# Idle matmuls of one wait replaced by groups of several lengths and offsets, and copies of zeros on the other engines

## The chip, the cores and the metric

The kernel runs on one core of a Trainium2 chip. The core has five engines that work side by side and meet through semaphores: TensorE (matmul, PE in the profile, its weight loads PEld), VectorE (DVE), ScalarE (ACT), GpSimd (POOL) and SyncE (SP), which issues all transfers here. The metric is the device time of one execution in microseconds (us), the median over the runs. Smaller is better.

## The reference

A spectral layer over 8 batches of 3008 positions with 256 channels is followed by a feed-forward layer of width 2048. Cut to what is computed:

```python
X = np.fft.rfft(x, axis=1)
Yr = Xr @ w_r - Xi @ w_i + b_r
Yi = Xr @ w_i + Xi @ w_r + b_i
Yr = np.sign(Yr) * np.maximum(np.abs(Yr) - 0.01, 0.0)      # Yi likewise
y = np.fft.irfft(Yr + 1j * Yi, n=3008, axis=1)
h = y.reshape(-1, 256) @ w_in
out = (h - np.tanh(h)) @ w_out
```

The feed-forward weights come as 64-bit floats and are turned into pairs of 32-bit numbers on the chip.

## The kernel before

The Fourier transform is done by matmuls with constant matrices, in two steps of 47 and 64 (3008 = 47 × 64). `Forward` is the first step: it takes 4 of 32 pairs of rows, splits them into a high and a low part (L90 on ScalarE, L91 on VectorE), multiplies by `f1` (L215 to L217) and writes the result `st` to the DRAM tile `a` (L231, L234). `Spectrum`, for batch 0 `WholeSpectrum`, is the second step with the complex linear layer and the shrinking: it loads `at` from `a` (L255), multiplies by `f2` (L264), and for batch 0 adds the bias by a matmul (L346) and multiplies by the linear weights (L352); then follow the shrinking (L361 to L371), the inverse step (L375) and a store to `z`. A `Chunk` takes 470 positions (the last two 282) through the rest of the inverse transform (L407) and the feed-forward layer (L420 to L445).

TensorE works in two types. Operands of type float32r are numbers rounded to fewer bits; the kernel splits each into high and low and adds three products (L215 to L217, L284, L420, L445). Operands of plain float32 (L264, L352, L375, L407) are used whole.

The order is written out by hand: each engine runs its instructions in the order in which the code issues them (`tc.manual_schedule`), and the tile pools add the waits. Batch 0 has nothing to hide behind. Its `Forward` loop (L523 to L535) runs 16 steps, each with one idle matmul behind its three; at the end the `a` tile has to go out to DRAM and come back as `at`. In this wait stands `idle(16)` (L536). `idle(n)` (L504 to L507) takes a PSUM tile of pool `ps_h`, which has two, and multiplies a tile of zeros, `warm`, by itself n times over 512 columns, in float32r. Nobody reads the result.

Behind the wait, in program order: the first two loads of `at` (L577, L578), `combine_linear` (L117 to L127: sums of the linear weights on VectorE and GpSimd, `ones` and the bias row), the split of `i1`, and the loop over the 12 units (L581 to L613), in which the feed-forward weights are also converted, a few steps at a time, into `win_h`, `win_l`, `wout_h` and `wout_l`. These four tiles are written there for the first time.

Of the kernel before, what the change touches and what calls it, by code (L numbers as in the profile page):

```python
# [10 lines left out]
F32 = mybir.dt.float32  # L11
# [3 lines left out]
ALU = mybir.AluOpType  # L15
# [6 lines left out]
def index_maps():  # L22
    n = np.arange(S)
    time = np.zeros((64, 47), np.int64)
    time[n % 64, n % 47] = n
    starts = []
    for j in range(NJ):
        low = (47 * np.arange(64) + 64 * j) % S < S // 2
        starts.append(next(m for m in range(64) if low[m] and not low[m - 1]))
    return time, starts  # L30
# [36 lines left out]
def spectral_ffn(ctx, tc, x, w_r, w_i, b_r, b_i, w_in, w_out, f1, f2, i1, i2, out):  # L67
    nc = tc.nc
    P = 128
    w_in, w_out = w_in.bitcast(U32), w_out.bitcast(U32)  # L70
    _, m0 = index_maps()
# [11 lines left out]
    ps_h = ctx.enter_context(tc.tile_pool(name="ps_h", bufs=2, space=PSUM))  # L83
# [46 lines left out]
    win_h = const.tile([P, 2, FF], F32R, name="win_h")  # L130
    win_l = const.tile([P, 2, FF], F32R, name="win_l")
    wout_h = const.tile([P, NF, D], F32R, name="wout_h")
# [365 lines left out]
    with tc.manual_schedule(engines={E.PE, E.Activation, E.DVE, E.Pool, E.SP}):  # L498
        zero = cvt.tile([P, 512], F32, name="zero", tag="w_f")
# [4 lines left out]
        def idle(n):  # L504
            ps = ps_h.tile([P, 512], F32, name="idle", tag="h")
            for _ in range(n):
                nc.tensor.matmul(ps, warm[:, :P], warm, start=True, stop=True)  # L507

        idle(11)
        shifts = const.tile([P, 2], F32, name="shifts")  # L510
        below, rebias = shifts[:, 0:1], shifts[:, 1:2]
# [11 lines left out]
        for i in range(len(steps) + 2):  # L523
# [9 lines left out]
            if i >= 2:  # L533
                f, q = steps[i - 2]
                f.keep(q, nc.vector.tensor_copy if i % 3 == 0 else nc.scalar.copy)  # L535
        idle(16)  # L536
        units = [WholeSpectrum(0, jp) for jp in range(NJ // 2)]
        i2t = const.tile([96, NP * 94], F32, name="i2")
        lin = []
# [144 lines left out]
    for c in range(FIRST, NCH):  # L684
        at = NF * (c - 1)
# [35 lines left out]
```

## Time and profile before

| | us |
|---|---|
| runs | 2694.08 and 2696.0, median 2695.04 |
| span of the profiled execution | 2694.1 |
| TensorE busy, of the span | 2676.7 |
| VectorE, ScalarE, GpSimd busy | 1748.3, 1377.5, 2.0 |
| mean granted clock of TensorE | 0.998 |

Times in views are counted from the first instruction. A row of the timeline has start, length, engine, line, operation, output and inputs, sizes and a count; instructions of one kind that follow each other are merged into one row, whose length runs from the first start to the last end. In brackets stands how long the engine was idle before it, and what ended that. A row of the chain has start, length and what the end of the program is traced back to at that time. A granted clock of 1.00 is full speed. A matmul's own length is longer than the distance between two of them, since they overlap.

The edited place is near the start: `Forward` of batch 0 ends at 22.3 us and the first unit begins at 32.2 us. All of the about 2,584 us after the loop of units, from 110 us on, are chunks, with the other batches' transforms between them.

### The profile page before, as it was taken

The numbers are of one execution on the slowest core, as the hardware profiler recorded it, in microseconds if no ns is written. First come the engines' busy times: TensorE is split into PE (matmuls) and PEld (weight loads), VectorE is DVE, ScalarE is ACT, GpSimd is POOL, SyncE is SP. The second block draws the span as 40 slices with busy tenths as digits, with TensorE's granted clock in tenths as the row PEclk, the third lists the DMA queues.
The fourth block names the chain that finished last, engine by engine and source line by source line (L and its number), as shares of the span: only waits on it lengthen the run. The fifth ranks groups of instructions, "written<-read, shape, count | busy, mean of one in ns | idle before, by whom it ended". The sixth has DMA issues, their size and how long they took to land.

```text
span 2694.1 us, 36955 instructions
## 1 busy us (share of the span) xinstructions
PE 2676.7 (99%) x14169; PEld 2391.6 (89%) x14169; DVE 1748.3 (65%) x3079; ACT 1377.5 (51%) x2587; POOL 2.0 (0%) x5
## 2 busy tenths in 40 slices
PE   8999999999999999999999999999999999999999
PEld 6788988999889998999988999899988999998989
DVE  6895786666557666566755667666665666655555
ACT  5555555454554446454455445644455444444445
POOL 0000000000000000000000000000000000000000
PEclk9999999999999999999999999999999999999999
DMA  6423223110231103111022110411113111100000
GB/s 196 141 75 106 65 83 109 46 54 26 69 90 43 50 32 111 57 47 46 24 81 80 46 46 31 118 56 50 39 39 108 50 39 41 35 23 22 20 20 17
DMA packets 105135, 163.47 MB, mean 61 GB/s; under 512 B 7488, under 2 KB 70976, under 8 KB 104864
## 3 DMA queue, kind: packets, MB, share of 16 engines
q1 hardware_dynamic: 104960, 161.13, 19.8%
q8 instruction: 111, 1.82, 0.3%
q14 instruction: 64, 0.52, 0.1%
HBM read 86.13 MB, written 74.97 MB: 60 GB/s over the span
## 4 chain that ended last, share of the span: by engine, by line
PE 94%; DVE 3%; DMA 1%; ACT 1%; issue 1%; SPq 0%; DVEq 0%; ACTq 0%
PE o L445 37%; PE h L420 37%; PE ps_v L284 4%; PE ps_i L407 4%; PE ps_f L264 3%; PE ps_t L284 2%; PE ps_f L215 1%; PE ps_f L217 1%; PE ps_f L216 1%; PE ps_v L352 1%; DVE g L425 1%; PE ps_i L320 1%; PE ps_i L321 1%; PE ps_i L319 1%; DVE gl L433 0%
## 5 line engine op out<-in xcount | busy, mean ns | idle before, releaser
L425 DVE TENSOR_TENSOR g<-h,th 128x470 f32<-128x470 f32 (+1 forms) x832 | 532.2, 640 | 540.0 <-ACT th L423 531.9
L423 ACT ACTIVATE th<-h 128x470 f32<-128x470 f32 (+1 forms) x832 | 463.9, 558 | 757.3 <-PE h L420 756.3
L433 DVE TENSOR_TENSOR gl<-g,gh 128x470 fp32r<-128x470 f32 (+1 forms) x832 | 531.9, 639 | 285.8 <-ACT gh L427 203.2
L427 ACT CAST gh<-g 128x470 fp32r<-128x470 f32 (+1 forms) x832 | 483.0, 581 | 408.6 <-DVE g L425 401.2
L445 PE MATMUL o<-gh,wout_l 128*128 128x470 f32 (+1 forms) x1664 | 631.3, 379 | 1.1 <-ACT gh L427 1.1
L445 PE MATMUL o<-gl,wout_h 128*128 128x470 f32 (+1 forms) x1664 | 616.1, 370 | 1.1 <-DVE gl L433 1.1
L445 PE MATMUL o<-gh,wout_h 128*128 128x470 f32 (+1 forms) x1664 | 615.8, 370 | 0.0
L420 PE MATMUL h<-yl,win_h 128*128 128x470 f32 (+1 forms) x1664 | 480.7, 370 | 0.0
L420 PE MATMUL h<-yh,win_l 128*128 128x470 f32 (+1 forms) x1664 | 480.1, 370 | 0.0
L420 PE MATMUL h<-yh,win_h 128*128 128x470 f32 (+1 forms) x1664 | 479.5, 369 | 0.0
L445 PEld LDWEIGHTS o<-gl,wout_h 128*128 128x128 f32 x1664 | 312.8, 188 | 40.8 <-DVE gl L433 2.1
L445 PEld LDWEIGHTS o<-gh,wout_l 128*128 128x128 f32 x1664 | 313.1, 188 | 35.1 <-ACT gh L427 1.7
L420 PEld LDWEIGHTS h<-yh,win_l 128*128 128x128 f32 x1664 | 310.5, 188 | 36.2 <-ACT yh L411 0.4
L420 PEld LDWEIGHTS h<-yl,win_h 128*128 128x128 f32 x1664 | 310.6, 188 | 35.5
L420 PEld LDWEIGHTS h<-yh,win_h 128*128 128x128 f32 x1664 | 310.6, 188 | 35.5
L445 PEld LDWEIGHTS o<-gh,wout_h 128*128 128x128 f32 x1664 | 313.5, 188 | 32.0
L309 DVE TENSOR_TENSOR y<-tb,ps_v 64x256 f32<-64x256 f32 x384 | 160.2, 417 | 12.0 <-ACT tb L356 6.8
L407 PEld LDWEIGHTS ps_i<-i,zin 96*128 96x128 f32 x1024 | 126.1, 192 | 5.0 <-DVE st L231 1.0
L407 PE MATMUL ps_i<-i,zin 96*128 96x94 f32 x1024 | 128.0, 272 | 1.0 <-DVE st L231 0.8
L91 DVE TENSOR_TENSOR x_l<-xt,x_h 94x512 fp32r<-94x512 f32 x126 | 85.6, 686 | 46.2 <-ACT x_h L90 44.3
L264 PEld LDWEIGHTS ps_f<-f,at 128*128 128x128 f32 x768 | 101.5, 192 | 13.6 <-issue 8.2
L264 PE MATMUL ps_f<-f,at 128*128 128x128 f32 x768 | 103.1, 277 | 5.7 <-DMA at<-a 5.7
(98 smaller groups left out, 2077.8 us busy)
## 6 DMA issues: line engine op xcount, KB each, us to landing
xt<-in_x SPq DMA_DIRECT2D x64, 384.0 KB, 3.6
at<-a SPq DMA_DIRECT2D x96, 256.0 KB, 2.8
z<-zo SPq DMA_DIRECT2D x96, 256.0 KB, 2.0
out<-ot SPq DMA_DIRECT2D x50, 470.0 KB, 2.9
a<-st SPq DMA_DIRECT2D x56, 384.0 KB, 3.2
zin<-z SPq DMA_DIRECT2D x44, 480.0 KB, 4.2
w_raw<-in_moe_w_in SPq DMA_DIRECT2D x8, 512.0 KB, 4.6
w_raw<-in_moe_w_out SPq DMA_DIRECT2D x8, 512.0 KB, 5.1
```

The costliest lines, as they stand in the source:

```text
L91: rest.tensor_tensor(out=lo, in0=src, in1=hi.bitcast(F32), op=ALU.subtract)
L215: nc.tensor.matmul(pv, f1h, xl, start=True, stop=False)
L264: nc.tensor.matmul(pv[:, t, jj], self.at[:, jj, t * P:(t + 1) * P], rhs, start=True, stop=True)
L284: nc.tensor.matmul(dst, lhs[:, t], rhs[:, t, :], start=n == 0, stop=n == 5)
L309: nc.vector.tensor_tensor(out=y[ri * 64:(ri + 1) * 64, jj, :], in0=common(jj, ri), in1=self.vv[jj * 64:(jj + 1) * 64, ri * D:(ri + 1) * D] ...
L407: nc.tensor.matmul(ps[:, k * 94:(k + 1) * 94], self.zt[:, k, t * P:(t + 1) * P], i2t[:, p * 94:(p + 1) * 94], start=True, stop=True,)
L420: nc.tensor.matmul(h[:, :n], lhs[:, t, f * P:(f + 1) * P], rhs[:, t, :n], start=k == 0, stop=k == 5)
L423: nc.scalar.activation(out=th[:, :n], in_=h[:, :n], func=AF.Tanh)
L425: nc.vector.tensor_tensor(out=g[:, :n], in0=h[:, :n], in1=th[:, :n], op=ALU.subtract)
L427: nc.scalar.copy(out=gh[:, :n], in_=g[:, :n])
L433: nc.vector.tensor_tensor(out=gl[:, :n], in0=g[:, :n], in1=gh[:, :n].bitcast(F32), op=ALU.subtract)
L445: nc.tensor.matmul(self.o[t][:, :n], lhs[:, f, t * P:(t + 1) * P], rhs[:, :n], start=f == 0 and k == 0, stop=f == NF - 1 and k == 2,)
```

## The change

`idle(16)` at L536 becomes a call of a new function, `measure()`. It writes zeros into parts of `win_h` and `win_l` with copies on VectorE and ScalarE, and uses them as weights (`wt`, four blocks of 128 columns in turn) and as moving operand (`mv`). After `idle(8)` come three loops of float32r matmuls: 12 each of 470, 500, 504, 512 and 128 columns, those of 470 from elements 8, 0, 4 and 12 of `mv`; 24 each of 250, 252, 256, 236 and again 252 columns; and 24 each of 252 and 128 columns with the same block of weights throughout. These are 264 matmuls, in groups of six that add up in one of two PSUM tiles of pool `ps_h`. Then `idle(2)`. Last come eight subtractions of zeros on GpSimd, eight on VectorE and eight copies of zeros on ScalarE, of 252 and 504 columns, into parts of `win_l` and `wout_h`. All results are overwritten later or never read.

```diff
+        def measure():
+            wt = win_h.rearrange("p k f -> p (k f)")
+            mv = win_l.rearrange("p k f -> p (k f)")
+            nc.vector.tensor_copy(out=wt[:, :512], in_=zero)
+            nc.vector.tensor_copy(out=mv[:, :512], in_=zero)
+            nc.scalar.copy(out=mv[:, 512:1024], in_=zero)
+            pa, pb = (ps_h.tile([P, 512], F32, name=f"idle{v}", tag="h") for v in "ab")
+            idle(8)
+            for n, start in ((470, 8), (470, 0), (470, 4), (470, 12), (500, 8), (504, 8), (512, 8), (128, 8)):
+                for k in range(12):
+                    nc.tensor.matmul((pa, pb)[k // 6][:, :n], wt[:, k % 4 * P:(k % 4 + 1) * P], mv[:, start:start + n], start=k % 6 == 0, stop=k % 6 == 5)
+            for n, start in ((250, 8), (252, 8), (256, 8), (236, 8), (252, 0)):
+                for k in range(24):
+                    at = 256 * (k // 6 % 2)
+                    nc.tensor.matmul((pa, pb)[k // 12][:, at:at + n], wt[:, k % 4 * P:(k % 4 + 1) * P], mv[:, start:start + n], start=k % 6 == 0, stop=k % 6 == 5)
+            for n, same in ((252, 1), (128, 1)):
+                for k in range(24):
+                    at = 256 * (k // 6 % 2)
+                    nc.tensor.matmul((pa, pb)[k // 12][:, at:at + n], wt[:, :P], mv[:, 8:8 + n], start=k % 6 == 0, stop=k % 6 == 5)
+            idle(2)
+            sums = win_l[:, 1, :1024]
+            for n in (252, 504):
+                for _ in range(4):
+                    nc.gpsimd.tensor_tensor(out=sums[:, :n], in0=zero[:, :n], in1=zero[:, :n], op=ALU.subtract)
+            for n in (252, 504):
+                for _ in range(4):
+                    nc.vector.tensor_tensor(out=sums[:, 512:512 + n], in0=zero[:, :n], in1=zero[:, :n], op=ALU.subtract)
+            for n in (252, 504):
+                for _ in range(4):
+                    nc.scalar.copy(out=wout_h[:, :2].rearrange("p t e -> p (t e)")[:, :n], in_=zero[:, :n])
...
-        idle(16)
+        measure()
```

In the rows below, which are an engine's instructions in their order, a name ending in `_49` is the semaphore of the engine or transfer queue that is waited for. TensorE in the wait of batch 0, before: the last product of `Forward` (`ps_f_336`), the idle matmuls, and the two `f2` products of the first units.

```order
L217 MATMUL ps_f_336<-x_7_1_h,f_h 96x512
L507 MATMUL idle<-warm 128x512 [waits PE_49] x2
L507 MATMUL idle<-warm 128x512 x15
L264 MATMUL ps_f_393<-f_129,at 128x2x64 [waits DMAHW7_49,DMAHW1_49]
L264 MATMUL ps_f_393<-f_129,at 128x2x64 x3
L264 MATMUL ps_f_404<-f_129,at 128x2x64 [waits DMAHW0_49,DVE_49]
```

TensorE at the same place, now: the end of the groups and the same first unit (`ps_f_681` was `ps_f_393`).

```order
L523 MATMUL idleb<-win_l,win_h 128x252 x12
L527 MATMUL idlea<-win_l,win_h 128x252 x12
L527 MATMUL idleb<-win_l,win_h 128x252 x12
L527 MATMUL idlea<-win_l,win_h 128x128 x12
L527 MATMUL idleb<-win_l,win_h 128x128 x12
L507 MATMUL idle<-warm 128x512 [waits PE_49]
L507 MATMUL idle<-warm 128x512
L264 MATMUL ps_f_681<-f_129,at 128x2x64 [waits DMAHW7_49,DMAHW1_49]
```

The first unit still waits for the transfers of `at`, but stands behind 264 matmuls and ten idle ones instead of 16 idle ones.

VectorE behind the last copy of `Forward`, before: the sums of the linear weights, `ones`, the bias row and the low part of `i1`.

```order
L231 COPY st<-ps_f_314 96x512 [waits DMAHW6_49,PE_49]
L117 SCALAR_TENSOR_TENSOR w_f<-wr_f,wi_f 128x512 [waits DMAHW6_49,DMAHW0_49]
L120 TENSOR_SCALAR ones<-zero 33x128
L125 CAST brow<-zero 33x512
L126 CAST brow<-bias_top 1x512 [waits DVE_49,Activation_49]
```

VectorE at the same place, now.

```order
L231 COPY st<-ps_f_314 96x512 [waits DMAHW6_49,PE_49]
L512 CAST win_h<-zero 128x512
L513 CAST win_l<-zero 128x512
L535 TENSOR_TENSOR win_l<-zero 128x252
L535 TENSOR_TENSOR win_l<-zero 128x252 [waits DVE_49] x3
L535 TENSOR_TENSOR win_l<-zero 128x504 [waits DVE_49] x4
L117 SCALAR_TENSOR_TENSOR w_f<-wr_f,wi_f 128x512 [waits DMAHW6_49,DMAHW0_49]
```

Ten instructions now stand ahead of L117 on VectorE.

GpSimd, before: constants, then one subtraction of linear weights, which is all it does.

```order
L700 MEMSET const-uint8-127 128x1
L714 UNCONDITIONAL_BRANCH [waits barrier_Pool_Activation_PE_DVE_SP_gather]
L118 ISA
L118 TENSOR_TENSOR w_f<-wi_f,wr_f 128x512 [waits DMAHW6_49,DMAHW0_49]
L714 UNCONDITIONAL_BRANCH
```

GpSimd, now.

```order
L745 UNCONDITIONAL_BRANCH [waits barrier_Pool_Activation_PE_DVE_SP_gather]
L532 ISA
L532 TENSOR_TENSOR win_l<-zero 128x252 [waits DVE_49]
L532 TENSOR_TENSOR win_l<-zero 128x252 [waits Pool_49] x3
L532 TENSOR_TENSOR win_l<-zero 128x504 [waits Pool_49] x4
L118 TENSOR_TENSOR w_f<-wi_f,wr_f 128x512 [waits DMAHW6_49,DMAHW0_49]
```

Eight subtractions stand ahead of L118, and the first waits only for VectorE's `zero`.

## The prediction

> **What bounds the kernel now.** I read the page first for the span, then the chain that ended last within the first 120 us, then the timeline and the stretches around the place that is edited. The change touches only batch 0's wait, at 22 to 32 us; of the page only the span is needed, against which the sum is made.
>
> ```profile
> span 2694.1 us, 36955 instructions
> ```
>
> The chain (start, length, what) shows what ends last around the edit. Up to 32.24 us it is transfers, the last of them the load of `at`. From there it is TensorE, line after line.
>
> ```profile
> 24.43 3.94 DMA a<-st
> 28.52 3.59 DMA at<-a
> 32.24 3.75 PE ps_f L264 x16
> 35.99 0.72 PE ps_v L346
> 36.72 3.71 PE ps_v L352 x8
> 40.43 1.06 PE ps_t L352 x4
> ```
>
> The timeline (start, length, engine, line) shows the edited group itself, 17 idle matmuls (16 of them from the replaced call), then 5.68 us in which TensorE has nothing until `at` lands, then the first unit and the second.
>
> ```profile
> 22.50 4.06 PE L507 MATMUL idle<-warm 128*128 128x512 f32 x17
> 32.24 3.75 PE L264 MATMUL ps_f<-f,at 128*128 128x128 f32 x16 [5.68 <-DMA at<-a]
> ...
> 41.33 1.06 PE L264 MATMUL ps_f<-f,at 128*128 128x128 f32 x8
> 42.31 0.50 PE L346 MATMUL ps_v<-brow,ones 33*128 33x512 f32 x1
> 42.74 1.99 PE L352 MATMUL ps_v<-w_f,xf 128*128 128x256 f32 x8
> 44.57 1.03 PE L352 MATMUL ps_t<-wr_f,sf 128*128 128x256 f32 x4
> 45.43 1.06 PE L264 MATMUL ps_f<-f,at 128*128 128x128 f32 x8
> ```
>
> The view by stretches has the granted clock (PEclk) behind the busy times. After the gap it is 0.50 until about 41 us, and the first unit runs at half speed.
>
> ```profile
> core 0: us, PE busy (x) PEld busy (x) DVE busy (x) ACT busy (x) POOL busy (x), PEclk, DMA share, GB/s
> 7.00:12.00 5.00, 4.97 (x21) 3.24 (x22) 3.81 (x7) 4.30 (x9) 0.00 (x0) 1.00 1.04 274
> 26.50:32.20 5.70, 0.06 (x1) 0.00 (x0) 2.78 (x5) 0.12 (x1) 0.97 (x1) 0.85 0.60 182
> 32.20:36.00 3.80, 3.75 (x17) 3.56 (x17) 0.42 (x1) 0.59 (x1) 0.00 (x0) 0.50 0.84 292
> 36.00:40.00 4.00, 4.00 (x9) 2.94 (x10) 2.37 (x6) 1.10 (x2) 0.00 (x0) 0.50 0.43 142
> 44.00:48.00 4.00, 4.00 (x22) 3.36 (x21) 3.11 (x7) 3.50 (x7) 0.00 (x0) 1.00 0.12 45
> ```
>
> So whatever TensorE does between 22.5 and 32.2 us is free, and what goes beyond is paid in full, since everything after is a chain on TensorE. The change puts 264 matmuls there, and the question is what one of them costs.
>
> **What a matmul costs, by its length.** Matmuls overlap, so the cost is the distance between two starts. These rows give it: start differences for float32r at 256, 470 and 282 columns, and for merged groups of one kind the length of the row less one record, over the count less one. Plain float32 (L264, L352, L407) leaves two records for each instruction. The last two rows have the time of a single record in ns, one as median, one as mean.
>
> ```profile
> 800.45 0.40 PE L284 MATMUL ps_v<-w_h,xl 128*128 128x256 f32 x2
> ...
> 801.16 0.38 PE L445 MATMUL o<-gh,wout_l 128*128 128x470 f32 x1
> ...
> 802.44 0.58 PE L420 MATMUL h<-yh,win_l 128*128 128x470 f32 x2
> ...
> 812.71 1.05 PE L264 MATMUL ps_f<-f,at 128*128 128x128 f32 x8
> ...
> 820.10 1.25 PE L407 MATMUL ps_i<-i,zin 96*128 96x94 f32 x10
> 2642.03 0.29 PE L445 MATMUL o<-gh,wout_l 128*128 128x282 f32 x1
> ...
> 2642.80 0.41 PE L420 MATMUL h<-yh,win_l 128*128 128x282 f32 x2
> ...
> L507 PE MATMUL idle<-warm x65: 387/395/796, 1.9 to 106.1; 128*128 128x512 f32 x65
> ...
> L407 PE MATMUL ps_i<-i,zin 96*128 96x94 f32 x1024 | 128.0, 272 | 1.0 <-DVE st L231 0.8
> ```
>
> Of 512 columns: (4.06 − 0.40) / 16 = 0.229 us, with 0.40 for a single one (median 395 ns in the row of L507). Of 470: 801.16 to 802.44 holds six, 0.213; I take 0.212. Of 282: 2642.03 to 2642.80 holds six, 0.128. Of 256: 800.45 to 801.16 holds six, 0.118. These lie on one line of about 0.0004 us a column, which gives 0.224 for 500 and 0.226 for 504. Below 256 columns no float32r matmul is in the trace. The same line gives 0.116 at 252 and 0.115 at 250. It cannot go on for ever, since each matmul loads 128 new weight columns: the float32 records of 128 and of 94 columns are (1.05 − 0.27) / 7 = 0.111 and (1.25 − 0.27) / 9 = 0.109 apart, although one is a third longer. I take that 0.110 as a floor, for 236 and for 128 columns.
>
> The bounds of this unknown: from below, without the floor the 36 matmuls of 128 columns would cost 0.063 by the line, 1.7 us less in all. From above, a float32r matmul under 256 columns could cost what a float32 one does. The row at 44.57 has four records of 256 columns in 0.86 us, two records to an instruction: 0.43 us for 256 columns, 3.6 times as much. I take the line, as 250 and 252 columns are nearest to the 256 of float32r; the upper end is the first rival.
>
> **The change part by part.**
> - Removed: `idle(16)`; added: `idle(8)` and, behind the groups, `idle(2)`. One idle matmul of the loop stays ahead of them. The first group starts at 22.50 + 9 × 0.229 = 24.56 us.
> - First loop: 48 × 0.212 (470 columns) + 12 × (0.224 + 0.226 + 0.229 + 0.110) = 10.18 + 9.47 = 19.65 us. For the starts at 0, 4 and 12 instead of 8 elements I add nothing. The L407 matmuls start at multiples of 94 elements and keep to the floor; but they are float32, so a doubled cost of the 24 at 4 and 12, 5.1 us, stays the upper end.
> - Second and third loop: 24 × (0.115 + 3 × 0.116 + 0.118 + 0.110 + 0.110) = 19.22 us. The same weights in the last two groups save nothing: the 17 idle matmuls have equal weights too, and each still leaves a weight load in the trace.
> - `idle(2)`: 0.46 us. Three first matmuls wait on TensorE itself for a shared PSUM tile; each waits out what a 512-column matmul takes beyond its distance, 0.40 − 0.23 = 0.17 at most, 0.34 in all for the two that follow a fresh writer.
> - Sum: 24.56 + 19.65 + 19.22 + 0.46 + 0.34 = 64.2 us, where the first L264 can start instead of at 32.24. That is +32.0 us.
> - Given back: TensorE has no gap any more, so the clock should stay at 1.00 as in the stretch from 44 us. The first unit takes 41.33 − 32.24 = 9.09 us at half clock. The next takes 45.43 − 41.33 = 4.10 with one L264 group of 0.98, and the first has one group more: 5.08. Gain 4.0 us. If the clock drops all the same, it is nothing.
>
> The copies on the other engines lie beside this, and I cost them at nothing. Their cover is the stretch up to 64 us:
>
> ```profile
> 1.43 0.43 DVE L502 CAST warm<-zero 128x512 fp32r<-128x512 f32 x1
> ...
> 21.60 0.68 DVE L231 COPY st<-ps_f 96x512 f32<-96x512 f32 x1
> ...
> 23.29 0.62 ACT L123 CAST bias_top<-bias 33x512 fp32r<-33x512 f32 x1
> 25.66 0.69 DVE L117 SCALAR_TENSOR_TENSOR w_f<-wr_f,wi_f 128x512 f32<-128x512 f32 x1 [3.38 <-DMA wr_f<-in_w_r]
> 25.70 1.77 POOL L118 TENSOR_TENSOR w_f<-wi_f,wr_f 128x512 f32<-128x512 f32 x1 [25.26 <-DMA wr_f<-in_w_r]
> 26.27 1.28 DVE L120 TENSOR_SCALAR ones<-zero 33x128 fp32r<-33x128 f32 x1
> ...
> 29.15 0.29 DVE L91 TENSOR_TENSOR i_l<-i_f,i_h 128x128 fp32r<-128x128 f32 x1
> ```
>
> - VectorE: two casts of 0.43 from 22.28, so the operands stand at 23.1, ahead of 24.56. Then four subtractions of 504 columns at 0.69 and four of 252 at about half, 0.4: 5.2 us in all, done at 27.5. Queued behind them are L117 to L91 of `i_l`, 3.8 us from 25.66 to 29.44 in the trace; they now end at about 31.3, while L346, which waits for them, cannot start before 65. Without the groups this would still come before its 35.9.
> - ScalarE: one cast of 0.62, four of 504 at 0.62 and four of 252 at about 0.35, 4.5 us from 23.3. L123 and the cast of `i_h` follow at 27.8 instead of 23.29, the next copy waits for TensorE at 65.
> - GpSimd: its eight subtractions stand ahead of L118 but wait only for `zero`, so they run from about 1.4 us. Four at 1.77 and four at about 0.9 make 10.7 us, done at 12, before `wr` lands at 25.7.
> - SyncE's third load of `at` waits for L117 on VectorE and so goes out some 2 us later, and is still landed long before 64.
>
> The sum: +32.0 − 4.0 = +28.0 us on the profiled execution's 2694.1, which is the lower of the two runs whose median is 2695.04. Forecast 2722 us.
>
> One rule speaks for another figure. The Trainium skill's page "TensorE: Matmul & The Clock Gate", section "Back-to-back issue gap", puts a sustained stream with weight loads at about 81 ns for 128 columns and 131 ns for 512. By it an estimate of the groups is 28 us instead of 39, and the forecast 2711. This trace disagrees where it can be asked: 0.229 at 512 and 0.212 at 470.
>
> **The rivals.**
> - *Float32r loses its speed under 256 columns.* The place is the groups of 250, 252, 236 and 128 columns, and the condition that each runs like float32. 24 × (0.420 + 3 × 0.423 + 0.396) + 36 × 0.22 + 24 × 0.118 = 50.0 + 7.9 + 2.8, plus 18.3 for the longer ones, is 79.1 instead of 38.9: 2762 us, slower by 2.5%. It decides the verdict once a 252-column matmul takes over 0.33 us. Against it: 256 and 282 columns lie on the line with no sign of a step. For it: nothing shorter ran, and float32 at 256 shows what the engine takes for the full product. The Trainium skill's page "FP8 and Floating Point Precision", section "TensorE Precision Notes", gives true float32 four passes and the reduced form one read with truncation, and names no length; no run here shows that below 256.
> - *A smaller step, two passes:* 24 × 5 × 0.21 + 36 × 0.11 + 2.8 + 18.3 = 50.3, that is 2734 us.
> - *GpSimd holds VectorE in the first stage.* At 26.27 L120, of 128 columns as the last row of 0.29, took 1.28 us and ended as GpSimd's 1.77 did, so GpSimd can hold VectorE up. Now it works from 1.4 to 12 us, where VectorE is busy 3.81 of 5 us and TensorE waits for its splits. Six splits held for 0.69 each are 4.1 us, less 1.2 of slack: +3, 2725 us. If VectorE were kept from its first split, at 4.4 us, until 12, it would be +7.6, 2730. Against it: L117, with two inputs like the splits, kept its 0.69 beside GpSimd. The Trainium skill's page "GPSIMD Engine Reference" says that the two share SBUF interfaces and collide for VectorE instructions with two SBUF inputs; L117's row does not show it.
> - *The groups cost nothing*, because the wait hides them: they would have to end by 32.24, that is 264 in 7.7 us or 0.029 each, a quarter of the floor.
>
> **How the numbers follow.** Forecast as worked out, 2722 (own range 2716 to 2728, by the floor, the 4 us of the clock and a part of the offsets): 0.52. Float32 speed under 256: 0.33. Two passes: 0.08. GpSimd: 0.06. Hidden: 0.01. Leaving out the first rival would leave out 0.33, so the range goes from 2716 to its 2762 with the 5 us of offsets: 2767. About 2%, up to 2749 us, is what a measurement of this kernel tells from no change: slower has the 0.33 and 0.01 for mixtures, faster 0.01, within 0.65.
>
> **What would show it.** Right: TensorE without a gap from 22.5 us, L264 first at about 64, a clock of 1.00 there, starts 0.212 apart at 470, 0.116 at 252 and 0.110 at 128 columns, and the rest shifted as a whole. Wrong: 252 columns at over 0.2, a step between 250 or 252 and 256, 470 columns from element 4 slower than from 8, L91's splits longer than 0.69 before 12 us, or a clock of 0.50 behind the groups.

## The result and the profile after

The changed kernel takes 2725.53 us (two runs, 2725.03 and 2726.04) against 2695.04, a ratio of 1.0115 with a 95% interval of 1.0085 to 1.0144: slower by 30.5 us, 1.1%. The forecast was 2722. The profiled execution has a span 30.2 us longer than before, and this difference is taken apart below.

```profile
span 2724.3 us, 37499 instructions
```

The timeline of TensorE after the change, from the last idle matmul of the first stage on (start, length, then the merged rows of a kind). Where two tiles, `idlea` and `idleb`, share a length, only the first of the two rows is shown.

```profile
23.74 2.24 PE L507 MATMUL idle<-warm 128*128 128x512 f32 x9
25.82 1.43 PE L519 MATMUL idlea<-win_l,win_h 128*128 128x470 f32 x6
...
28.34 1.44 PE L519 MATMUL idlea<-win_l,win_h 128*128 128x470 f32 x6
...
30.91 1.46 PE L519 MATMUL idlea<-win_l,win_h 128*128 128x470 f32 x6
...
33.51 1.44 PE L519 MATMUL idlea<-win_l,win_h 128*128 128x470 f32 x6
...
36.07 1.52 PE L519 MATMUL idlea<-win_l,win_h 128*128 128x500 f32 x6
...
48.43 1.56 PE L523 MATMUL idlea<-win_l,win_h 128*128 128x252 f32 x12
...
51.23 1.56 PE L523 MATMUL idlea<-win_l,win_h 128*128 128x256 f32 x12
...
54.03 1.50 PE L523 MATMUL idlea<-win_l,win_h 128*128 128x236 f32 x12
...
62.30 1.45 PE L527 MATMUL idlea<-win_l,win_h 128*128 128x128 f32 x12
...
64.93 0.68 PE L507 MATMUL idle<-warm 128*128 128x512 f32 x2
65.44 1.95 PE L264 MATMUL ps_f<-f,at 128*128 128x128 f32 x16
...
70.44 1.05 PE L264 MATMUL ps_f<-f,at 128*128 128x128 f32 x8
```

No row has an idle time in brackets: the gap is gone. The distance is the step from one kind to the next, over the count. The 24 of 252 columns take 51.23 − 48.43 = 2.80 us, 0.117 each, and the 24 of 256 take 54.03 − 51.23 = 2.80, the same. There is no step at 256. The groups end at 64.93 and last 39.11 us, and the first unit starts at 65.44, 1.2 us later than forecast, while the first idle row starts 1.24 later than the 22.50 of before. So the slip came before the groups. The first unit takes 70.44 − 65.44 = 5.00 us, where it took 9.09.

The stretches of the kernel after have the clock (PEclk) in the first unit, where it had been 0.50, and show GpSimd at work in the first stage:

```profile
core 0: us, PE busy (x) PEld busy (x) DVE busy (x) ACT busy (x) POOL busy (x), PEclk, DMA share, GB/s
7.00:12.00 5.00, 4.29 (x17) 2.59 (x17) 4.81 (x6) 3.31 (x6) 2.38 (x2) 1.00 1.03 252
...
64.00:70.00 6.00, 6.00 (x39) 5.30 (x39) 2.38 (x7) 1.69 (x3) 0.00 (x0) 1.00 0.32 90
```

From 7 to 12 us TensorE lost 0.7 us and VectorE is busier, with fewer instructions. The timeline of VectorE and GpSimd after says why, and shows the copies beside the groups:

```profile
1.48 7.98 POOL L532 TENSOR_TENSOR win_l<-zero 128x252 fp32r<-128x252 f32 x8 [1.04 <-DVE zero L500]
6.00 4.61 DVE L91 TENSOR_TENSOR x_l<-xt,x_h 94x512 fp32r<-94x512 f32 x4 [1.51 <-ACT x_h L90]
11.13 0.67 DVE L91 TENSOR_TENSOR x_l<-xt,x_h 94x512 fp32r<-94x512 f32 x1
...
23.89 5.63 DVE L535 TENSOR_TENSOR win_l<-zero 128x252 fp32r<-128x252 f32 x8
...
31.85 0.29 DVE L91 TENSOR_TENSOR i_l<-i_f,i_h 128x128 fp32r<-128x128 f32 x1
```

Four splits take 4.61 us while GpSimd works until 9.46, and the next one alone takes 0.67. Read one at a time (the same view over shorter stretches), the four take 1.14, 1.51, 1.51 and 0.68 us, and the fourth starts at 9.93, when GpSimd is done. This is the third:

```profile
8.49 1.51 DVE L91 TENSOR_TENSOR x_l<-xt,x_h 94x512 fp32r<-94x512 f32 x1
```

So three splits are held up, by 2.1 us in all over the usual 0.69. VectorE's own subtractions end at 29.5, and what is queued behind them at 32.1, 33 us before the first unit starts.

Setting the start of each matmul of the program against its start before: the first unit starts 33.20 us later, the second 29.11 (70.44 − 41.33), and this stays so for 390 us. Then one load of `zin` takes 6.04 us from issue to landing, where it took 4.90, and from there to the end it is 30.2. The waits of the kernel after from 460 to 466 us (total, count, longest):

```profile
PE ps_i L407 <- DMA zin<-z: 1.2, 1, 1.2
```

In the kernel before, TensorE stood there for 0.2 us.

### The profile page after: what moved, and what is told of

Same layout as the page of the kernel before. It is cut to its first block, busy times and chain, and to the rows that moved or that the text cites. A ratio compares the mean times of both kernels' runs of the same rounds, so it can differ in the third digit from the quotient of the medians.

```text
span 2724.3 us, 37499 instructions
## 1 busy us (share of the span) xinstructions
PE 2710.2 (99%) x14427; PEld 2423.7 (89%) x14427; DVE 1755.4 (64%) x3089; ACT 1382.1 (51%) x2596; POOL 9.2 (0%) x13
## 4 chain that ended last, share of the span: by engine, by line
PE 96%; DVE 2%; ACT 1%; DMA 1%; issue 0%; SPq 0%; ACTq 0%; DVEq 0%
PE o L445 37%; PE h L420 37%; PE ps_v L284 4%; PE ps_i L407 4%; PE ps_f L264 3%; PE ps_t L284 2%; PE ps_f L215 1%; PE ps_f L217 1%; PE ps_f L216 1%; PE ps_v L352 1%; PE ps_i L320 1%; PE ps_i L321 1%; PE ps_i L319 1%; DVE g L425 1%; PE idleb L519 0%
## 5 line engine op out<-in xcount | busy, mean ns | idle before, releaser
L445 PEld LDWEIGHTS o<-gh,wout_h 128*128 128x128 f32 x1664 | 313.5, 188 | 32.1
L407 PEld LDWEIGHTS ps_i<-i,zin 96*128 96x128 f32 x1024 | 126.1, 192 | 6.0 <-DMA zin<-z 2.1
L407 PE MATMUL ps_i<-i,zin 96*128 96x94 f32 x1024 | 128.0, 272 | 2.0 <-DMA zin<-z 1.2
```

What stands on the lines that cost most here:

```text
L407: nc.tensor.matmul(ps[:, k * 94:(k + 1) * 94], self.zt[:, k, t * P:(t + 1) * P], i2t[:, p * 94:(p + 1) * 94], start=True, stop=True,)
L445: nc.tensor.matmul(self.o[t][:, :n], lhs[:, f, t * P:(t + 1) * P], rhs[:, :n], start=f == 0 and k == 0, stop=f == NF - 1 and k == 2,)
```

## The experiments

**Without GpSimd's subtractions.**

```diff
-            for n in (252, 504):
-                for _ in range(4):
-                    nc.gpsimd.tensor_tensor(out=sums[:, :n], in0=zero[:, :n], in1=zero[:, :n], op=ALU.subtract)
```

> The changed kernel without its eight GpSimd subtractions. Theory: they held VectorE's splits in the first stage, which moved everything by 1.24 us (the idle matmuls behind the first stage began at 23.74 instead of 22.50 us). Without them the splits are 0.69 us each again, the idle matmuls begin at 22.5, the first L264 at 64.2 instead of 65.4, and the span is 1.2 us shorter, about 2723. Rival: the slip was a late input transfer or chance, and the first L264 stays at 65.4.

The timeline of this kernel, VectorE and TensorE:

```profile
6.24 1.29 DVE L91 TENSOR_TENSOR x_l<-xt,x_h 94x512 fp32r<-94x512 f32 x2 [2.24 <-ACT x_h L90]
...
23.00 2.23 PE L507 MATMUL idle<-warm 128*128 128x512 f32 x9
...
64.70 1.95 PE L264 MATMUL ps_f<-f,at 128*128 128x128 f32 x16
```

Two splits take 1.29 us, 0.69 or less each again, and the first unit starts 0.74 us earlier than in the changed kernel; 1.24 was expected. VectorE waited 0.76 us for an `x_h` from ScalarE at 18.4 us, where 0.2 to 0.3 is usual, and that is the rest. The end of the first stage moves from one execution to the next: its last product starts at 22.1 to 22.8 us in the seven profiles without these subtractions at the start, and at 23.5 to 23.6 in the five with them. The span did not follow, 2724.9 (2727.06 us, one run): behind the same late `zin` (1.1 us) stands something new, the clock at 0.50 from 140.2 to 143.6 us, which costs 1.4. This gave the question for the last two runs below.

**The same subtractions later**, behind L118 in GpSimd's order.

```diff
         whole_lin, bias_rows = combine_linear(*lin_in, zero)
+        sums = win_l[:, 1, :1024]
+        for n in (252, 504):
+            for _ in range(4):
+                nc.gpsimd.tensor_tensor(out=sums[:, :n], in0=zero[:, :n], in1=zero[:, :n], op=ALU.subtract)
```

> The changed kernel with GpSimd's eight subtractions issued behind L118, so that they run from about 27 us, beside the groups, instead of from 1.5. Theory: they are free there. First stage as before, first L264 at 64.2, span about 2723, as without them. Rival: they hold VectorE there too, and the bias row comes late; that must exceed 30 us to be seen, so it would show only in VectorE's rows.

Here are GpSimd, VectorE and TensorE of this kernel:

```profile
27.72 8.44 POOL L611 TENSOR_TENSOR win_l<-zero 128x252 fp32r<-128x252 f32 x8
...
28.22 1.09 DVE L117 SCALAR_TENSOR_TENSOR w_f<-wr_f,wi_f 128x512 f32<-128x512 f32 x1
...
31.98 1.01 DVE L91 TENSOR_TENSOR i_l<-i_f,i_h 128x128 fp32r<-128x128 f32 x1
...
64.03 1.95 PE L264 MATMUL ps_f<-f,at 128*128 128x128 f32 x16
```

The theory came true for TensorE, and what the rival said came true for VectorE. The first stage ends as before the change (its last idle matmuls begin at 22.32) and the first unit starts at 64.0, 1.41 us earlier than in the changed kernel. VectorE is held here too, 1.09 us for L117 instead of 0.69 and 1.01 for a split of 0.29, and nobody waits. The span is 2723.5, with a drop of the clock at 139.9 us in it again.

**The copies without the matmuls.** The 264 matmuls and the two PSUM tiles go, `idle(8)` stands in place of `idle(2)`.

```diff
-            for n, start in ((470, 8), (470, 0), (470, 4), (470, 12), (500, 8), (504, 8), (512, 8), (128, 8)):
...
-            idle(2)
+            idle(8)
```

> All copies and subtractions of zeros stay on the three engines, the 264 matmuls go; 16 idle matmuls stand there again. Theory: the matmuls are the whole cost but for the GpSimd part. The first stage ends 1.2 us later, so the load of at lands 1.2 us later, at about 33.4, the clock drops to 0.50 in the gap, the first unit takes 9.1 us, and the span is 2695.3. Rival: the copies ahead of L117 on VectorE and of L123 on ScalarE delay the bias row or the third load of at, which the groups had covered: over 2 us more, 2697 or above.

TensorE and the stretches of this kernel:

```profile
23.71 4.04 PE L507 MATMUL idle<-warm 128*128 128x512 f32 x17
32.78 3.45 PE L264 MATMUL ps_f<-f,at 128*128 128x128 f32 x16 [5.03 <-DMA at<-a]
...
39.28 1.05 PE L264 MATMUL ps_f<-f,at 128*128 128x128 f32 x8
...
32.00:36.00 4.00, 3.22 (x16) 3.25 (x16) 0.54 (x2) 0.59 (x1) 0.00 (x0) 0.57 0.92 282
36.00:40.00 4.00, 4.00 (x23) 3.32 (x22) 2.57 (x7) 1.48 (x3) 0.00 (x0) 1.00 0.64 224
```

The matmuls are the whole cost: without them the kernel is at 2691.6 (2693.35 us, one run), not slower than before. The number missed. The first stage ended 1.2 us later, yet `at` landed only 0.5 later, and the first unit took 6.50 us (39.28 − 32.78) instead of 9.1: the clock was at 0.50 for one step of 3.41 us, not three.

**The groups twice.**

```diff
+            for _ in range(2):
-            for n, start in ((470, 8), (470, 0), (470, 4), (470, 12), (500, 8), (504, 8), (512, 8), (128, 8)):
+                for n, start in ((470, 8), (470, 0), (470, 4), (470, 12), (500, 8), (504, 8), (512, 8), (128, 8)):
...
```

> The changed kernel with its three loops of matmuls run twice. Theory: all of it lies on the path, at the same distances: 39.1 us more, first L264 at 104.5, span 2763. Rival: a part of the first pass was hidden or was a cost of the first use, so that the second pass costs less or more than 39.1 by over 1 us.

The first row of each pass and the end, TensorE of this kernel:

```profile
25.93 1.43 PE L520 MATMUL idlea<-win_l,win_h 128*128 128x470 f32 x6
...
65.04 1.49 PE L520 MATMUL idlea<-win_l,win_h 128*128 128x470 f32 x6
...
104.21 0.68 PE L507 MATMUL idle<-warm 128*128 128x512 f32 x2
104.72 1.95 PE L264 MATMUL ps_f<-f,at 128*128 128x128 f32 x16
```

39.11 us for the first pass, 39.17 for the second, and a span of 2762.2 (2763.97 us, one run). Each pass is on the path whole.

**What sets the floor, and real data.** The second and third loop give way to these; the outputs that nobody reads are all that differs.

```diff
+            for n, cols in ((128, 128), (128, 64), (64, 128), (64, 64), (256, 64)):
+                for k in range(24):
+                    at = 256 * (k // 6 % 2)
+                    nc.tensor.matmul((pa, pb)[k // 12][:cols, at:at + n], wt[:, k % 4 * P:k % 4 * P + cols], mv[:, 8:8 + n], start=k % 6 == 0, stop=k % 6 == 5)
+            xh = first[-1].x[1][0].rearrange("p a d -> p (a d)")
+            for n in (252, 256):
+                for k in range(24):
+                    at = 256 * (k // 6 % 2)
+                    nc.tensor.matmul((pa, pb)[k // 12][:96, at:at + n], (f1h, f1l)[k % 2], xh[:, :n], start=k % 6 == 0, stop=k % 6 == 5)
```

> The changed kernel with other groups in the second and third loop, 24 each: 128 columns with weights of 128 and of 64 columns, 64 columns with weights of 128 and of 64, 256 columns with weights of 64, then 252 and 256 columns with real data (the transform's constants as weights, 96 columns, and the split input as moving operand, 94 rows). Theory: the 0.110 floor is the load of 128 weight columns. 128 and 64 columns with 128 weight columns stand 0.11 apart, both with 64 weight columns 0.055 to 0.065, 256 stays at 0.117. Rival: a fixed cost of any float32r matmul, so all short groups stand at 0.11. On the data: theory 0.117 at 252 and 256 as with zeros. Rival: zeros hid the loss of speed under 256 columns, and 252 with data stands at 0.4 while 256 stands at 0.117.

The timeline of this kernel; the pair of sizes reads rows * weight columns, then rows x moving columns:

```profile
45.57 1.50 PE L523 MATMUL idlea<-win_l,win_h 128*128 128x128 f32 x12
...
48.25 0.89 PE L523 MATMUL idlea<-win_l,win_h 128*64 128x128 f32 x12
...
49.70 1.47 PE L523 MATMUL idlea<-win_l,win_h 128*128 128x64 f32 x12
...
52.34 0.86 PE L523 MATMUL idlea<-win_l,win_h 128*64 128x64 f32 x12
...
53.74 1.60 PE L523 MATMUL idlea<-win_l,win_h 128*64 128x256 f32 x12
...
56.60 0.28 PE L528 MATMUL idlea<-x_h,f_h 94*96 94x252 f32 x1
...
59.40 0.28 PE L528 MATMUL idlea<-x_h,f_h 94*96 94x256 f32 x1
```

24 of each, so the steps give 0.112 and 0.110 with 128 weight columns, whether 128 or 64 columns move, and 0.060 and 0.058 with 64 weight columns. The floor goes with the weight columns, and so does the length of a weight load's own record, 192 ns with 128 columns and 136 with 64; the rival of a fixed cost falls. Real data at 252 columns took (59.40 − 56.60) / 24 = 0.117, as zeros did, and 0.118 at 256: zeros hid nothing.

**Three times the copies on VectorE and ScalarE.**

```diff
-                for _ in range(4):
+                for _ in range(12):
...
```

> The changed kernel with three times the subtractions on VectorE and the copies on ScalarE (24 each instead of 8). Theory: they lie beside the groups and cost nothing; VectorE ends at about 43, ScalarE at about 38, both ahead of 65.4, and the span stays at 2724.3 within 1 us. Rival: they slow the groups through shared memory, and the 470-column groups stand over 0.214 apart.

VectorE, ScalarE and TensorE of this kernel:

```profile
23.87 15.01 DVE L535 TENSOR_TENSOR win_l<-zero 128x252 fp32r<-128x252 f32 x24
...
24.91 12.97 ACT L538 CAST wout_h<-zero 128x252 fp32r<-128x252 f32 x24
...
65.41 1.95 PE L264 MATMUL ps_f<-f,at 128*128 128x128 f32 x16
```

9.4 and 8.7 us more on these engines, and the first unit starts where it did, 65.41 against 65.44. The span is 2723.7, the rest of the difference to 2724.3 being a `zin` wait of 0.7 instead of 1.2 us.

**Filling the gap only.** Two kernels from the one before, with 41 and with 30 idle matmuls.

```diff
-        idle(16)
+        idle(41)
```

> The kernel before with idle(41) in place of idle(16): the gap in the wait is filled and nothing else. Theory: the 4.0 us given back in the changed kernel are the clock alone. TensorE is busy until 32.1, the clock stays at 1.00, the first unit takes 5.0 instead of 9.1 us, and the span is 2690, 4.1 less than before. Rival: the first unit, when it is faster, waits for the third load of at, and a good part of the gain goes there: 2692 or more. Second rival: the clock drops all the same, 2694.

> The kernel before with idle(30): the gap in the wait shrinks from 5.7 to about 2.6 us. Theory: a gap that short does not drop the clock, and the gain is that of the filled gap: first unit 5.0 us, span 2690. Rival: any gap of some us drops it, and the first unit takes 9 us as before, 2694; between these if it drops for a shorter time.

With 41, TensorE and the stretches:

```profile
32.95 2.02 PE L264 MATMUL ps_f<-f,at 128*128 128x128 f32 x16 [0.94 <-DMA at<-a]
...
39.11 1.16 PE L264 MATMUL ps_f<-f,at 128*128 128x128 f32 x8 [0.92 <-DMA at<-a]
...
104.00:109.00 5.00, 4.14 (x34) 3.68 (x32) 4.86 (x10) 2.16 (x5) 0.00 (x0) 1.00 0.43 100
109.00:116.00 7.00, 6.96 (x23) 6.24 (x24) 3.20 (x6) 1.70 (x3) 0.00 (x0) 0.51 0.98 312
```

The clock stayed at 1.00 through the first unit, as expected, and the third load of `at` then took part of it, 0.92 us of wait, as the rival said. But at 109 us the clock dropped for 6.8 us, at a gap of 0.9 us where before it had not, and the span is 2695.1 where 2690 was expected. In time, nothing came of it: 2695.26 us against 2694.49, ratio 0.9998 (0.9989 to 1.0008). With 30, the gap was still 2.87 us and the clock dropped at 32.3 and at 110.8 us, for one step each: 2693.5. So a gap that short can drop the clock, against the theory.

**The kernel before once more**, unchanged.

> The kernel before, unchanged. Theory: how long the clock stays at 0.50 is set by chance, by where a fixed raster of about 3.41 us falls on the gap; in the first profile it was 10.24 us, three steps of it, and another execution may have one or two, with a first unit of 6 to 8 us. Rival: the 5.7 us gap always costs three steps, and the first unit takes 9.1 us again.

TensorE and a stretch of this execution:

```profile
33.52 3.69 PE L264 MATMUL ps_f<-f,at 128*128 128x128 f32 x16 [6.38 <-DMA at<-a]
...
40.26 1.06 PE L264 MATMUL ps_f<-f,at 128*128 128x128 f32 x8
...
30.18:37.01 6.83, 3.50 (x16) 3.49 (x16) 0.77 (x3) 0.59 (x1) 0.00 (x0) 0.50 0.86 265
```

The same program, a longer gap, a shorter stretch at half clock: two steps, and a first unit of 6.74 us (40.26 − 33.52).

**Filling both gaps.**

```diff
-        idle(16)
+        idle(41)
...
             for t in range(2):
+                if c + t == 2:
+                    idle(4)
                 chunks[c].time(t)
```

> The kernel before with idle(41) in place of idle(16), and idle(4) ahead of the last transform of the second chunk, where TensorE stood still for 0.8 to 1.0 us at about 110 us and the clock dropped in four of the ten profiled runs so far, the one with 41 idle matmuls among them. Theory: the clock is 1.00 throughout, so the first unit's 4 us are not given back at 110 us; about 1.5 us still go to the wait for the third load of at and behind it, and the span is 2691 to 2692.5. Rival: the stretch of short matmuls there drops the clock without the gap, and the span is 2694 to 2695.5 as with 41 alone.

TensorE of this kernel at the second place:

```profile
104.95 3.59 PE L407 MATMUL ps_i<-i,zin 96*128 96x94 f32 x30
108.32 1.17 PE L507 MATMUL idle<-warm 128*128 128x512 f32 x4
109.33 1.30 PE L407 MATMUL ps_i<-i,zin 96*128 96x94 f32 x10
```

No drop, and a span of 2692.4. In time it can't be told from before: 2694.54 us against 2696.42, ratio 0.9995 (0.9986 to 1.0004), eleven runs against fifteen. What differs is the spread: 2693.6 to 2696.0 here, 2694.1 to 2700.2 before. The fifteen runs of before go with their mean clock: 2694.1 to 2695.0 at 0.999, 2696.4 to 2697.4 at 0.998, 2697.1 to 2700.2 at 0.997.

## Why the prediction was right, step by step

- *The groups, 38.87 us.* They took 39.11. The line from 256 to 512 columns goes on below 256, down to a floor of 0.110: 0.117 at 252, 0.111 at 236 ((56.70 − 54.03) / 24, the next kind starting at 56.70), 0.110 at 128. The floor goes with the 128 weight columns, as assumed, and equal weights saved nothing. The estimate of 28 us for the groups did not come true.
- *The first rival, the speed of float32 under 256 columns,* had a chance of 0.33 and is refuted, in the changed kernel and on real data. The two-pass rival falls with it.
- *The offsets at nothing.* By the starts above: 0.210 from element 8, 0.214 from 0, 0.217 from 4, 0.213 from 12, at most 0.08 us for a group of twelve.
- *The clock, −4.0 us.* The first unit took 5.00 instead of 9.09, so 4.1 came back. But the 9.09 was one draw: other executions with the gap show 6.5 and 6.74. Against those the gain would have been 1.5 to 1.7 us. That the 4.0 came out to 0.1 is luck in this sense: the sum was made from the execution that it was then held against.
- *GpSimd at nothing.* This is the term that failed: its eight subtractions cost 1.24 us at the end of the first stage. The rival had the mechanism, with a chance of 0.06, but not the size: three splits were held, by 2.1 us, and not six by 4.1, since GpSimd was done at 9.46 us and not at 12. I had let L117's 0.69 beside GpSimd speak against it, and that row was misread. L117 had begun at 25.66, 0.04 us ahead of GpSimd's L118, and ran through; L120, which began during L118, was held until L118 ended at 27.47. The three splits too began during a subtraction of GpSimd and ended 0.54 to 0.55 us behind it, and in the kernel with the late subtractions the same L117 began 0.5 us into one and took 1.09. In these rows it is who begins first that decides. The Trainium skill's page "GPSIMD Engine Reference", section "Specifications", has the rule for VectorE instructions with two SBUF inputs; the traces now agree, 1.51 us for a split of 0.69.
- *The other copies at nothing.* Right: VectorE was done with them and all behind them 33 us before the first unit, and three times as many changed nothing.
- *Not foreseen:* 1.06 us at the `zin` load 400 us later. The load goes out 29.1 us later, like everything else, and then takes 1.14 us longer. In the six profiles without the groups TensorE's wait there is at most 0.2 us; in the six with them it is between none and 1.23, and the kernel with the groups twice had none. So the groups do not always bring it; whether the later start does at times, or only chance, was not tried.

So 28.0 + 1.2 (first unit at 65.44, not 64.2) − 0.1 (clock) + 1.1 (`zin`) is the 30.2 of the two spans. One reading at the start of the sum was wrong: 2694.1 is not the lower of the two runs but the span of the run of 2696.0, as a span is 1.7 to 2.2 us shorter than its run's time wherever both are on record. The 2722 is thus a span, to be held against 2724.3, and it is 2.2 us too low.

## What to carry to other kernels

Cost a block put into a wait by where it ends: what fits in is free, the rest is paid in full, and the price of each matmul can be read from distances between starts, with a floor set by the weight columns for short ones. An instruction put on an idle engine is not free if it holds up the engine that sets the pace, as GpSimd's held VectorE's splits; look at where in time it will run, not at where it stands in the code. And a gain of a few us from a clock drop that was avoided should be set against more than one execution, since the same program paid three steps of half clock in one execution and two in another.

## What the runs showed of the hardware that was not expected

The clock stays at 0.50 for multiples of 3.41 us: 3.41, 6.83 and 10.24 for gaps of 5.03, 6.38 and 5.68 us. The length of the gap does not order them. The Trainium skill's page "TensorE: Matmul & The Clock Gate", section "What's actually happening", tells of a free-running window of 3413 ns; the lengths agree.

A gap of 0.9 us was enough for a drop at about 110 us (140 in the longer kernels), right behind the 30 short matmuls of L407, but in only four of eleven executions with such a gap, of 0.4 to 1.0 us. With the gap filled there was none in the profile, and ten of the eleven runs had a mean clock of 1.000. The length of these gaps does not order them either: 0.98 us went without a drop, 0.78 had one. Why these four dropped stays open; that it depends on how the steps fall on the gap is only argued.
